# The second shifted copy of VectorE's key tiles made in place by an accumulating DMA, in a two-branch attention kernel with a planned order

## The chip, the cores and the metric

The kernel runs on one core of one Trainium2 chip. The metric is the device time of one execution in microseconds, as the median of several runs. The core has five engines that work side by side, each on its own in-order queue: TensorE (PE; PEld is its weight load), VectorE (DVE), ScalarE (ACT), GpSimd (POOL) and SyncE (SP, which here only issues DMAs).

## The reference

One input `x` of 2048 tokens by 512 goes through two attention branches, and a gate mixes the results. Branch A is linear attention; branch B is softmax attention, without a mask, with 32 heads of 16 columns:

```python
g = _sigmoid((x * gate_w).sum(-1, keepdims=True))
# A: phi(q), phi(k) = softmax(+-(q W)), softmax(+-(k W)); o = phi(q) (phi(k)^T v) / (phi(q) sum phi(k))
# B:
scores = jnp.einsum("bhqd,bhkd->bhqk", q, k) * (Dh ** -0.5)
p = _softmax(scores, axis=-1)
o = jnp.einsum("bhqk,bhkd->bhqd", p, v)
...
return g * a + (1 - g) * b
```

In branch B, 32 heads times 2048 x 2048 exponentials, 134 million, have to be taken. That is the bulk of the work.

## The kernel before

**Sets and key tiles.** Branch B is cut into 32 sets (`N_SETS`): four blocks of 512 queries, times four groups of eight heads, times two. A set holds four heads and 512 queries, and walks over 16 key tiles of 128 keys. For one key tile TensorE computes the scores of four heads into PSUM banks (L1231, `qk`), an engine turns them into exponentials in SBUF, and TensorE multiplies these by the values into the set's accumulator `psO` (L1282, `pv`), four matmuls for one round.

**Two engines take exponentials.** ScalarE does it with its exponential function, two instructions of 128 x 1024 a key tile, into an `E` tile (L1246, `exp`). VectorE has none. It takes a scaled score plus a bias as a 16-bit integer, so that the integer's bits, read as bf16, are roughly the exponential (L1251, `expd`, four instructions of 128 x 512 a key tile, into a `T` tile of 128 x 2048). To smooth the error of that, the kernel adds two shifted copies of the same integers: `T` plus 43 and `T` plus 85 (`SHIFT`), in two `TS` tiles, each multiplied by values that carry a weight of their own (`vS`). So a key tile of VectorE needs three rounds at L1282 (`T`, and twice `TS`), where one of ScalarE needs one round (`E`).

**Who makes the copies.** The first copy (43) is always VectorE's, one instruction of 128 x 2048 (L1263, `sh`). The second (85) is VectorE's or GpSimd's (L1266, `shp`): the planner picks one.

**The planner.** The order of all work on all engines is laid down when the program is built, by a scheduler in the file (`_Sched`). It gives each operation a duration (`occ`) and a latency, and places operations one after the other on the engine where they can start first. Whether a key tile goes to ScalarE or VectorE is open for the tiles in `DSET` (3, 5, 7, 9, 11, 13 in each set) and is decided as the plan grows. VectorE's tiles are offered in the order of `DSET`. `STYLES` is a table of random seeds, one for each 3 us of the plan, that vary the weights of these choices. The finished order is fixed; at run time an engine waits on semaphores wherever an instruction needs another engine's result, and everything queued behind it on that engine waits with it.

**The port rule in the planner.** VectorE's copies (kind `sh`) and GpSimd's operations are not allowed to overlap: each `sh` is planned after GpSimd's last operation, and each GpSimd operation waits for VectorE's last `sh` (`port`, and `o.deps.append(self.sh[-1])`).

**Buffers.** `T` tiles come from a ring of three, `TS` tiles from a ring of four. Of the eight PSUM banks one is `psO`; seven hold scores (`psR`): ScalarE takes them in pairs, VectorE one at a time. The same seven also serve the projections and branch A.

**Other work around it.** GpSimd also runs parts of branch A (L1080 to L1090), and weights the values for `vS` (L958). SP issues the transposing DMAs: at the end of a set `psO` is copied to `OT` by VectorE (L866), transposed by DMA to `OTT` (L1194), and normalised by VectorE (`rB` at L1172, `ob` at L1174).

Of the kernel before, what the change touches and what calls it, by code (L numbers as in the profile page):

```python
# [6 lines left out]
BF16 = mybir.dt.bfloat16  # L7
F32 = mybir.dt.float32
I16 = mybir.dt.int16
I32 = mybir.dt.int32  # L10
ACTF = mybir.ActivationFunctionType
ALU = mybir.AluOpType
# [12 lines left out]

VW = 18
NBANK = 7
DSET = (3, 5, 7, 9, 11, 13)
SHIFT = (0, 43, 85)
WB16 = (1.0, 0.79296875, 0.6328125)  # L30
ACC = 128.0 / math.log(2.0) * SCALE
# [13 lines left out]
NE_, NPH = 12, 6  # L45
WINDOW = 3.0
STYLES = (
# [14 lines left out]
LEAD = {"act": 1.1, "dve": 1.0}  # L62
NE = "dve"
PORT, LONG, NEAR, HOLD = 0.05, 0.8, 0.6, 3.0
SWITCH = 0.11
GAP, NEARBY = 0.02, 0.05
Q32, PSH, SHP = 1, 2, 1.88
PVS = 4.0
CONT = 3.0
PIECE = 4  # L70
DSTEP, DLAG = 3.6, 3.0
ND = lambda s: 6
HAM, CELLS = 3.413, 0.46
TOL0, TOL1, TOL2, TOL3 = 0.05, 0.1, 0.08, 0.1

# [33 lines left out]
class _Sched:  # L109
# [89 lines left out]
    def _earliest(self, o, at):  # L199
        if o.half is not None and self.last_mode == "row":  # L200
            at = max(max(self.rows[i] for i in o.half), self.last_start + GAP)
        if o.kind == "sh":
            at = max(at, self.port["pool"])
        elif o.eng == "pool" and self.sh:
            at = max(at, self.port["dve"], o.est)
            if o.occ > LONG and at > self.port["dve"] + NEAR:
                at = max(at, o.est + HOLD)
        return self._place(o, at)[0]
# [97 lines left out]
    def advance(self, until):  # L306
        ready, free, pend, order = self.ready, self.free, self.pend, self.order
        while self.left:
# [34 lines left out]
            if o.eng == "pe":  # L343
                sw = SWITCH if self.last_mode is not None and o.mode != self.last_mode else 0.0
                occ += sw
                self.last_mode = o.mode
                self.last_start = w + sw
                self.rows = [w + occ if o.half is None or i in o.half else max(x, self.last_start + GAP) for i, x in enumerate(self.rows)]
            elif o.eng == "pool":
                if self.sh and self.sh[-1] not in o.deps and self.sh[-1].end > w - 20.0:  # L350
                    o.deps.append(self.sh[-1])
                self.port["pool"] = w + occ + PORT
            elif o.kind == "sh":
                self.sh.append(o)
                self.port["dve"] = w + occ + PORT
# [160 lines left out]
def _general(fast):  # L516
# [8 lines left out]
        return _Slots(r.aps)  # L525

    xT, Wp, W_Av, WAT, kz, kvs = ns.xT, ns.Wp, ns.W_Av, ns.WAT, ns.kz, ns.kvs
    T = [x.bitcast(BF16) for x in ns.T_r.aps + ns.TS_r.aps]
    M_r = _Slots([ns.banks[:, i, :] for i in (4, 5, 6)])
    S_r = _Slots([ns.banks[:, 0:4, :]])  # L530
    st_r, ss_r = _Slots([x[:, 0, :] for x in ns.ss_r.aps]), _Slots([x[:, 1, :] for x in ns.ss_r.aps])
# [182 lines left out]
def _build(ctx, nc, A_x, A_wqkv, A_w_phi, A_wo, B_wqkv, B_wo, gate_w, out):  # L714
    cnt = [0]

    def sb(shape, dt=BF16, name="sb"):
        cnt[0] += 1
        return ctx.enter_context(nc.sbuf_tensor(f"{name}_{cnt[0]}", shape, dt))

    def ring(n, shape, dt=BF16, name="r"):
        return _Slots([sb(shape, dt, name)[:] for _ in range(n)])
# [26 lines left out]
    ct = sb([128, 112], F32, name="ct")  # L749
    flag = sb([128, 1], I32, name="flag")  # L750
    shc = sb([128, 2], I32, name="shc")

    qst_r = ring(2, [128, NQ], name="qst")
    qz_r = ring(2, [128, 4, NQ], name="qz")
    E_r = ring(NE_, [128, 1024], name="E")
    T_r = ring(3, [128, 2048], I16, name="T")
    TS_r = ring(4, [128, 2048], I16, name="TS")
    phk_r = ring(NPH, [128, 1024], name="phk")
    vA_r = ring(4, [128, 8, 66], name="vA")
    oAT_r = ring(2, [128, KT, NQ], name="oAT")  # L760
# [78 lines left out]
    z4 = pool(-99.3, 0.2, lambda e: e.tensor_tensor(ta, ta, tb, ALU.mult), [z3])  # L839
    op_qm = pool(-99.2, 0.2, lambda e: e.tensor_tensor(qmask[:], ta[:, 0:4], ta[:, 4:8], ALU.add), [z4])  # L840
    op_shc = [pool(-99.04, 0.1, lambda e, m=m: e.memset(shc[:, m:m + 1], SHIFT[m + 1] * 65537)) for m in range(2)]
    op_zeros = pool(-99.03, 0.1, lambda e: e.memset(zeros[:], 0.0))
    op_ones = pool(-99.05, 0.3, lambda e: e.memset(ones[:], 1.0))
    op_qz0 = [pool(-60, 1.8, lambda e: e.memset(qz_r.aps[1 - q_t[0, 0].idx], 0.0))]
# [358 lines left out]
    for s in range(N_SETS):  # L1203
# [12 lines left out]
        for eng, frac, kt in todo:  # L1216
            alt = (((s, kt), eng),) if kt in dset else ()
            pr = st_(s + frac)
            T, T1, T2 = (_Tile(T_r), _Tile(TS_r), _Tile(TS_r)) if eng == "dve" else (None, None, None)
            exps, es = [], []  # L1220
            for cc in range(2):
                rs = [_Tile(B_r), _Tile(B_r)]
# [32 lines left out]
            if eng == "act":  # L1255
                rounds = [(exps, lambda cc, es=es: es[cc].ap, lambda hd, kt=kt: vB[:, kt, hd, :], [], es)]
            else:
                di = DSET.index(kt)
                sh = []
                for m, X in ((1, T1), (2, T2)):  # L1260
                    two = m >= PSH
                    a2 = lambda eng: alt + ((("sh", s, kt, m), eng),) if two else alt
                    sh.append([add("dve", pr + 1.0 + 0.3 * m, 0.6, lambda e, T=T, X=X, m=m: e.tensor_single_scalar(  # L1263
                        X.ap, T.ap, SHIFT[m], ALU.add), deps=exps, tiles=[T, X], name="sh", kind="sh", alt=a2("dve"))])
                    if two:
                        sh[-1].append(pool(pr + 1.0 + 0.3 * m, SHP, lambda e, T=T, X=X, m=m: e.tensor_tensor(  # L1266
                            X.ap.bitcast(I32), T.ap.bitcast(I32), shc[:, m - 1:m].to_broadcast([128, 1024]), ALU.add),
                            exps + op_shc, "shp", [T, X], a2("pool")))
                s1, s2 = sh
                rounds = [(exps, lambda cc, T=T: T.ap[:, 1024 * cc:1024 * (cc + 1)].bitcast(BF16), lambda hd, kt=kt: vB[:, kt, hd, :], [], [T]),  # L1270
                          (s1, lambda cc, T=T1: T.ap[:, 1024 * cc:1024 * (cc + 1)].bitcast(BF16),
                           lambda hd, di=di: vS[:, 0, di, hd, :], [op_vS[g, kt // 4, 0]], [T1]),
                          (s2, lambda cc, T=T2: T.ap[:, 1024 * cc:1024 * (cc + 1)].bitcast(BF16),
                           lambda hd, di=di: vS[:, 1, di, hd, :], [op_vS[g, kt // 4, 1]], [T2])]
            for ri, (dps, rhs, lhs, more, holds) in enumerate(rounds):
                def pv(e, rhs=rhs, lhs=lhs, g=g, par=par, O=O, s=s, key=(kt, ri)):
                    ins = None
                    for cc in range(2):
                        for h in range(2):
                            col = 2 * h + cc  # L1280
                            hd = 8 * g + 4 * h + 2 * cc + par
                            ins = e.matmul(O.ap[32 * col:32 * col + VW, :], lhsT=lhs(hd), rhs=rhs(cc)[:, 512 * h:512 * (h + 1)],  # L1282
                                           start=(first_pv[s] == key), stop=(last_pv[s] == key), tile_position=(0, 32 * col),
                                           skip_group_check=True)
                    return ins
                o = add("pe", pr + 2.5 - 40.0 * (s == N_SETS - 1), 0.22, pv, deps=list(dps) + [ev_v[g, kt // 4], op_psO] + more, tiles=holds + [O], mode="col",
                        name=f"pv{s}.{kt}.{ri}", kind="pv", alt=alt)
                o.run = (s, (kt, ri))
                set_O[s] = O
                pvs.append(o)  # L1290
# [170 lines left out]
```

## Time and profile before

| | |
|---|---|
| Median of 3 runs | 707.38 us (706.78 to 709.51) |
| Profiled execution, first to last instruction | 707.6 us |
| ACT busy | 679.7 us (96%) |
| DVE busy | 667.4 us (94%) |
| PE busy | 657.1 us (93%) |
| POOL busy | 429.3 us (61%) |
| Granted TensorE clock, mean | 0.990 |

The profiler gives no time for the profiled execution other than its span, 707.6 us. It is 0.2 us above the median of the runs, so nothing has to be added to the span to compare it with them. Busy time counts the time in which an engine has an instruction in hand; instructions that follow each other without a gap overlap a little, so a group's busy time is less than its count times the mean duration. For sums, the busy time divided by the count is used.

### The profile page before, as it was taken

The page shows a single profiled execution, that of the slowest core. Times are in us where ns is not written, and L with a number is a line of the kernel's source. Part 1 is how long each engine was busy: PE and PEld are TensorE (multiplying, and loading weights), DVE is VectorE, ACT ScalarE, POOL GpSimd, SP SyncE. Part 2 cuts the span into 40 slices and gives each one's busy share as a digit, 9 for nine tenths or more (in the row PEclk, how much of TensorE's full clock was granted, in tenths as well). Part 3 has the DMA queues.
Part 4 walks back from the last instruction along what each step waited for, and adds up shares of the span by engine and source line. Part 5 has one row for each costly group of instructions (what it writes and reads, how often), then busy time and mean ns, then how long its engine had stood idle before and what let it go on. Part 6 is the DMA issues. An engine that isn't in the chain of part 4 may idle for free.

```text
span 707.6 us, 16129 instructions
## 1 busy us (share of the span) xinstructions
PE 657.1 (93%) x6632; PEld 208.6 (29%) x6632; DVE 667.4 (94%) x1191; ACT 679.7 (96%) x769; POOL 429.3 (61%) x364
## 2 busy tenths in 40 slices
PE   8999999999999999989999999999999999988895
PEld 3333343332322222222222322222222222222222
DVE  5998899999999999999999999999999999999995
ACT  6999799999999999999999999999999999999994
POOL 5468666655756656656667766666666755566541
PEclk9999899999999999999999999999999999999998
DMA  6501000011000000102111121112212111220001
GB/s 145 154 16 10 13 12 16 17 59 25 10 16 16 9 17 8 24 8 36 34 31 38 46 54 28 40 40 45 38 31 47 42 32 35 38 45 9 16 9 34
DMA packets 72192, 23.80 MB, mean 34 GB/s; under 512 B 64048, under 2 KB 72112, under 8 KB 72112
## 3 DMA queue, kind: packets, MB, share of 16 engines
q1 hardware_dynamic: 70896, 21.93, 14.7%
q8 instruction: 53, 0.87, 0.6%
q10 hardware_dynamic: 1216, 0.79, 0.4%
q14 instruction: 27, 0.22, 0.1%
HBM read 4.21 MB, written 2.10 MB: 9 GB/s over the span
## 4 chain that ended last, share of the span: by engine, by line
ACT 77%; PE 15%; DVE 5%; DMA 1%; issue 0%
ACT E L1246 73%; PE psR L1231 5%; PE psO L1282 4%; PE psR L883 3%; DVE T L1251 3%; ACT phk L1074 2%; ACT WAT L1074 2%; PE psR L1326 1%; PE psR L945 1%; DMA OTT<-OT 1%; DVE TS L1263 1%; PE psR L897 1%; PE psR L1023 0%; DVE vB L950 0%; PE psR L1006 0%
## 5 line engine op out<-in xcount | busy, mean ns | idle before, releaser
L1246 ACT ACTIVATE E<-psR 128x1024 bf16<-128x1024 f32 x692 | 649.1, 1118 | 12.0 <-PE psR L1231 10.9
L1251 DVE TENSOR_SCALAR T<-psR 128x512 int16<-128x512 f32 x664 | 424.1, 678 | 19.9 <-PE psR L1231 16.5
L1231 PE MATMUL psR<-qz,kT 32*128 32x512 bf16 (+1 forms) x2048 | 294.0, 386 | 39.9 <-ACT E L1246 27.9
L1266 POOL TENSOR_TENSOR TS<-T,shc 128x1024 int32<-128x1024 int32 x127 | 240.4, 1893 | 94.9 <-DVE TS L1263 78.1
L1231 PEld LDWEIGHTS psR<-qz,kT 32*128 32x128 bf16 (+1 forms) x2048 | 77.6, 91 | 292.3 <-ACT E L1246 212.7
L1263 DVE TENSOR_SCALAR TS<-T 128x2048 int16<-128x2048 int16 x205 | 137.0, 683 | 0.4
L1282 PE MATMUL psO<-E,vB 128*18 128x512 bf16 x1384 | 126.1, 385 | 0.1
L1282 PE MATMUL psO<-TS,vS 128*18 128x512 bf16 x1328 | 122.1, 384 | 0.0
L1282 PE MATMUL psO<-T,vB 128*18 128x512 bf16 x664 | 65.6, 386 | 0.0
L1090 POOL TENSOR_TENSOR phk<-phk,ss 128x1024 bf16<-128x1024 bf16 x16 | 30.9, 1929 | 31.9 <-DVE TS L1263 31.9
L1085 POOL TENSOR_TENSOR tr<-WAT 128x256 f32<-128x256 f32 x32 | 23.3, 729 | 37.8 <-DVE TS L1263 37.8
L1090 POOL TENSOR_TENSOR WAT<-WAT,ss 128x1024 bf16<-128x1024 bf16 x16 | 30.9, 1929 | 25.2 <-DVE TS L1263 25.2
L1282 PEld LDWEIGHTS psO<-TS,vS 128*18 128x18 bf16 x1328 | 29.9, 88 | 54.8 <-issue 38.2
L1282 PEld LDWEIGHTS psO<-E,vB 128*18 128x18 bf16 x1384 | 31.6, 88 | 44.4 <-issue 31.0
L883 PE MATMUL psR<-xT,WB 128*128 128x512 bf16 x128 | 33.2, 383 | 0.4 <-ACT WAT L1074 0.3
L883 PE MATMUL psR<-Wp,xT 128*128 128x512 bf16 x128 | 33.2, 382 | 0.0
L1080 POOL TENSOR_TENSOR WAT<-WAT 128x512 f32<-128x512 bf16 x16 | 18.5, 1155 | 21.2 <-DVE TS L1263 16.3
L1282 PEld LDWEIGHTS psO<-T,vB 128*18 128x18 bf16 x664 | 16.2, 88 | 20.9 <-issue 17.0
L866 DVE CAST OT<-psO 128x512 bf16<-128x512 f32 x31 | 21.1, 682 | 0.1
L958 POOL TENSOR_SCALAR vS<-vB 128x144 bf16<-128x144 bf16 (+1 forms) x32 | 11.9, 373 | 14.4 <-DVE TS L1263 12.2
L1080 POOL TENSOR_TENSOR WAT<-phk 128x512 f32<-128x512 bf16 x16 | 18.5, 1156 | 2.9 <-DVE TS L1263 2.3
L1086 POOL TENSOR_TENSOR tr<-tr 128x128 f32<-128x128 f32 x32 | 12.8, 400 | 11.0 <-DVE TS L1263 9.4
(114 smaller groups left out, 412.2 us busy)
## 6 DMA issues: line engine op xcount, KB each, us to landing
qz<-qst SPq DMA_DIRECT2D x120, 16.0 KB, 1.8
out_dram<-WAv SPq DMA_DIRECT2D x12, 128.0 KB, 1.7
WB<-in_B_wqkv_dram SPq DMA_DIRECT2D x3, 384.0 KB, 5.3
T<-in_A_x_dram SPq DMA_DIRECT2D x2, 256.0 KB, 4.4
T<-in_A_x_dram ACTq DMA_DIRECT2D x2, 256.0 KB, 4.7
WAv<-in_A_wqkv_dram SPq DMA_DIRECT2D x1, 512.0 KB, 6.6
WB<-in_A_wo_dram SPq DMA_DIRECT2D x1, 512.0 KB, 3.4
WB<-in_B_wo_dram SPq DMA_DIRECT2D x1, 512.0 KB, 3.6
```

Of the source, the lines that this page charges most:

```text
L866: return add("dve", prio, 0.6, lambda e: e.tensor_copy(dst(), src()), deps=deps, tiles=tiles, name=name)
L883: calls = [lambda e, t=t: e.matmul(tile.ap[:, off:off + 512], lhsT=lhs(t), rhs=rhs(t), start=(t == 0), stop=(t == KT - 1)) for t in range(KT)]
L1074: ex = [add("act", prio, 0.48, lambda e, s=s: e.activation(ev()[:, :, 16 * s:16 * s + 16], P(), ACTF.Exp, scale=1.0 - 2.0 * s), deps=[f] + ...
L1080: p1 = pool(prio + 2, 1.23, lambda e: e.tensor_tensor(v8(), eg()[:, :, 0:8], eg()[:, :, 8:16], ALU.add), ex + use_wat, tiles=[ee, tr], nam ...
L1085: p2 = pool(prio + 2, 0.92, lambda e: e.tensor_tensor(u4(), v8()[:, :, 0:4], v8()[:, :, 4:8], ALU.add), [p1], tiles=[tr, tr2])
L1090: return pool(prio + 6, 1.95, lambda e: e.tensor_tensor(eg(), eg(), ss.ap[:, 1, :].unsqueeze(2).to_broadcast([128, 64, DH]), ALU.mult), [o ...
L1231: ins = e.matmul(rs[h].ap, lhsT=kT[a:a + n, g, 128 * kt:128 * (kt + 1)], rhs=qt.ap[a:a + n, c, :], start=True, stop=True, tile_position=(a ...
L1246: exps.append(add("act", pr + 0.5 * cc, 0.905, lambda e, rs=rs, E=E: e.activation(E.ap.rearrange("p (a n) -> p a n", n=512), pair(rs), ACT ...
L1251: exps.append(add("dve", pr + 0.5 * cc + 0.01 * h, 0.6, lambda e, rs=rs, T=T, cc=cc, h=h: e.tensor_scalar(T.ap[:, 1024 * cc + 512 * h:1024 ...
L1263: sh.append([add("dve", pr + 1.0 + 0.3 * m, 0.6, lambda e, T=T, X=X, m=m: e.tensor_single_scalar(X.ap, T.ap, SHIFT[m], ALU.add), deps=exps ...
L1266: sh[-1].append(pool(pr + 1.0 + 0.3 * m, SHP, lambda e, T=T, X=X, m=m: e.tensor_tensor(X.ap.bitcast(I32), T.ap.bitcast(I32), shc[:, m - 1: ...
L1282: ins = e.matmul(O.ap[32 * col:32 * col + VW, :], lhsT=lhs(hd), rhs=rhs(cc)[:, 512 * h:512 * (h + 1)], start=(first_pv[s] == key), stop=(l ...
```

## The change

- `DSET` has seven key tiles a set (1, 3, 5, 7, 9, 11, 13) instead of six, so `vS` holds seven weighted value tiles.
- For key tiles 1, 3, 5 and 7 (`BYDMA`), the second shifted copy is no longer an instruction. Once the first round has read `T`, and once the first copy has been made from it, GpSimd issues a DMA that adds a constant row of 85s, held in DRAM, to `T` in place. The third round then reads `T`. The tile needs two buffers instead of three.
- For those tiles the first copy may be VectorE's or GpSimd's. For 9, 11 and 13 it stays as it was: the first is VectorE's, the second either's.
- `T` and `TS` become one ring of seven.
- The DMA's issue counts 1.1 us of GpSimd (`SDO`) and 5.0 us of latency (`SDL`) in the planner, and is left out of the port rule (`o.dma is None`).
- `STYLES` is a new table, of 233 entries; before it had 232.

```diff
-DSET = (3, 5, 7, 9, 11, 13)
+DSET = (1, 3, 5, 7, 9, 11, 13)
...
-Q32, PSH, SHP = 1, 2, 1.88
+Q32, PSH, SHP = 1, 1, 1.88
+SDO, SDL = 1.1, 5.0
+BYDMA = (1, 3, 5, 7)
...
-ND = lambda s: 6
+ND = lambda s: 7
...
-        elif o.eng == "pool" and self.sh:
+        elif o.eng == "pool" and o.dma is None and self.sh:
...
-            elif o.eng == "pool":
+            elif o.eng == "pool" and o.dma is None:
...
+    step = sb([128, 16], I16, name="step")
+    step_d = nc.dram_tensor("shift_row", [128, 16], I16, kind="Internal").ap()
...
-    T_r = ring(3, [128, 2048], I16, name="T")
-    TS_r = ring(4, [128, 2048], I16, name="TS")
+    T_r = ring(7, [128, 2048], I16, name="T")
...
+    op_st = pool(-99.035, 0.1, lambda e: e.memset(step[:], SHIFT[2]))
+    op_std = dma("sp", -90.0, 3.0, step_d, step[:], deps=[op_st], name="step")
...
+                add_dma = kt in BYDMA
+                both = 1 if add_dma else 2
+                s1, s2 = [], []
+                for m, X, got in ((1, T1, s1), (2, T2, s2))[:both]:
+                    a2 = lambda eng: alt + ((("sh", s, kt, m), eng),) if m == both else alt
+                    got.append(add("dve", pr + 1.0 + 0.3 * m, 0.6, lambda e, T=T, X=X, m=m: e.tensor_single_scalar(
                         X.ap, T.ap, SHIFT[m], ALU.add), deps=exps, tiles=[T, X], name="sh", kind="sh", alt=a2("dve")))
+                    if m == both:
+                        got.append(pool(pr + 1.0 + 0.3 * m, SHP, lambda e, T=T, X=X, m=m: e.tensor_tensor(
                             X.ap.bitcast(I32), T.ap.bitcast(I32), shc[:, m - 1:m].to_broadcast([128, 1024]), ALU.add),
                             exps + op_shc, "shp", [T, X], a2("pool")))
+                if add_dma:
+                    T2 = T
...
+                if ri == 2 and add_dma:
+                    dps = [add("pool", pr + 1.6, SDO, lambda e, T=T: e.dma_start(T.ap, step_d.rearrange("p n -> (p n)").unsqueeze(0).to_broadcast([128, 2048]), accum_op=ALU.add), deps=[pv0, op_std] + s1,
+                               tiles=[T], name="shd", dma=SDL, lane=lambda T=T, key=(s, kt): (("shd", T.idx), key), alt=alt)]
                 o = add("pe", pr + 2.5 - 40.0 * (s == N_SETS - 1), 0.22, pv, deps=list(dps) + [ev_v[g, kt // 4], op_psO] + more, tiles=holds + [O], mode="col",
                         name=f"pv{s}.{kt}.{ri}", kind="pv", alt=alt)
+                if ri == 0:
+                    pv0 = o
```

More of the change, by code (lines that the diff above doesn't have):

```diff
@@ L527, in _general @@
     xT, Wp, W_Av, WAT, kz, kvs = ns.xT, ns.Wp, ns.W_Av, ns.WAT, ns.kz, ns.kvs
-    T = [x.bitcast(BF16) for x in ns.T_r.aps + ns.TS_r.aps]
+    T = [x.bitcast(BF16) for x in ns.T_r.aps]
     M_r = _Slots([ns.banks[:, i, :] for i in (4, 5, 6)])
@@ L1218, in _build @@
             pr = st_(s + frac)
-            T, T1, T2 = (_Tile(T_r), _Tile(TS_r), _Tile(TS_r)) if eng == "dve" else (None, None, None)
+            T, T1, T2 = (_Tile(T_r), _Tile(T_r), _Tile(T_r)) if eng == "dve" else (None, None, None)
             exps, es = [], []
@@ L1258, in _build @@
                 di = DSET.index(kt)
[L1259 to L1266, printed above, removed]
+                add_dma = kt in BYDMA
[4 more added lines that the diff above has]
+                    got.append(add("dve", pr + 1.0 + 0.3 * m, 0.6, lambda e, T=T, X=X, m=m: e.tensor_single_scalar(
+                        X.ap, T.ap, SHIFT[m], ALU.add), deps=exps, tiles=[T, X], name="sh", kind="sh", alt=a2("dve")))
+                    if m == both:
+                        got.append(pool(pr + 1.0 + 0.3 * m, SHP, lambda e, T=T, X=X, m=m: e.tensor_tensor(
                             X.ap.bitcast(I32), T.ap.bitcast(I32), shc[:, m - 1:m].to_broadcast([128, 1024]), ALU.add),
                             exps + op_shc, "shp", [T, X], a2("pool")))
-                s1, s2 = sh
+                if add_dma:
+                    T2 = T
                 rounds = [(exps, lambda cc, T=T: T.ap[:, 1024 * cc:1024 * (cc + 1)].bitcast(BF16), lambda hd, kt=kt: vB[:, kt, hd, :], [], [T]),
@@ L1274, in _build @@
                            lambda hd, di=di: vS[:, 1, di, hd, :], [op_vS[g, kt // 4, 1]], [T2])]
+            o = None
             for ri, (dps, rhs, lhs, more, holds) in enumerate(rounds):
```

27 rows, old and new, of the table STYLES are left out of this document.

## The prediction

> **What bounds the kernel now.** I read the page's busy times first, then the busy times by stretch, the groups, the waits, and the DMA issues.
>
> ```profile
> span 707.6 us, 16129 instructions
> PE 657.1 (93%) x6632; PEld 208.6 (29%) x6632; DVE 667.4 (94%) x1191; ACT 679.7 (96%) x769; POOL 429.3 (61%) x364
> ACT 77%; PE 15%; DVE 5%; DMA 1%; issue 0%
> ```
>
> Three engines are within 3% of each other, and the chain that ended last lies on ACT for 77% of the span. An average hides the stages, so here are the same busy times in three stretches (columns: length, PE, PEld, DVE, ACT, POOL, granted clock, DMA share, GB/s). The first row is a short stretch that I use further down.
>
> ```profile
> core 0: us, PE busy (x) PEld busy (x) DVE busy (x) ACT busy (x) POOL busy (x), PEclk, DMA share, GB/s
> 153.80:157.30 3.50, 3.50 (x46) 1.62 (x48) 3.31 (x7) 3.24 (x4) 1.53 (x3) 1.00 0.50 152
> ...
> 0.00:150.00 150.00, 143.47 (x1471) 56.47 (x1471) 134.56 (x239) 135.64 (x151) 94.02 (x103) 0.98 0.20 45
> 150.00:650.00 500.00, 466.13 (x4700) 138.18 (x4699) 485.38 (x870) 496.37 (x567) 312.94 (x251) 1.00 0.15 32
> 650.00:707.00 57.00, 47.52 (x472) 13.91 (x464) 47.46 (x84) 47.67 (x54) 22.32 (x12) 0.97 0.07 18
> ```
>
> From 150 to 650 us ACT is busy 496.4 of 500 us, and DVE 485.4. There, time falls only if exponentials leave ACT, and DVE has no room to take them unless something leaves DVE. In the first 150 us PE is the fullest, 143.5 against 135.6 for ACT. There, moving key tiles to DVE, which need more rounds of PE, gains nothing.
>
> ```profile
> L1246 ACT ACTIVATE E<-psR 128x1024 bf16<-128x1024 f32 x692 | 649.1, 1118 | 12.0 <-PE psR L1231 10.9
> L1251 DVE TENSOR_SCALAR T<-psR 128x512 int16<-128x512 f32 x664 | 424.1, 678 | 19.9 <-PE psR L1231 16.5
> ...
> L1266 POOL TENSOR_TENSOR TS<-T,shc 128x1024 int32<-128x1024 int32 x127 | 240.4, 1893 | 94.9 <-DVE TS L1263 78.1
> ...
> L1263 DVE TENSOR_SCALAR TS<-T 128x2048 int16<-128x2048 int16 x205 | 137.0, 683 | 0.4
> L1282 PE MATMUL psO<-E,vB 128*18 128x512 bf16 x1384 | 126.1, 385 | 0.1
> ```
>
> ACT's 692 instructions are 346 key tiles at 2 x 649.1/692 = 1.876 us. DVE's 664 are 166 tiles, 5.2 of the six offered in each of 32 sets, at 4 x 424.1/664 = 2.555 us. The 332 copies are split 205 on DVE, at 137.0/205 = 0.668 us, and 127 on GpSimd, at 1.893 us. A round of four matmuls at L1282 costs 4 x 126.1/1384 = 0.364 us of PE.
>
> **What the change takes off DVE.** VectorE's tiles are offered in the order of `DSET`, and the first four of the seven are now the DMA's. A set took 5.2 tiles, so I count all four in every set: 128 DMAs. With N tiles on DVE, and P copies on GpSimd, DVE keeps (N - 128) first copies of tiles 9 to 13 and N - P of the copies that either may make: S = 2N - 128 - P. How large P stays is decided by GpSimd's queue.
>
> ```profile
> POOL TS L1266 <- DVE TS L1263: 78.1, 53, 5.3
> ...
> POOL phk L1018 <- DVE TS L1263: 8.7, 4, 2.7
> ```
>
> These are the first and the last of nine rows of GpSimd's waits on DVE's copies; together they hold 236 of the 278 us that GpSimd is idle (707.6 - 429.3). They come from the port rule, which the next fence shows at work: DVE's copy ends at 303.51, and GpSimd's, which had been waiting 1.17 us, starts.
>
> ```profile
> 302.83 0.68 DVE L1263 TENSOR_SCALAR TS<-T 128x2048 int16<-128x2048 int16 x1
> ...
> 303.60 1.89 POOL L1266 TENSOR_TENSOR TS<-T,shc 128x1024 int32<-128x1024 int32 x1 [1.17 <-DVE TS L1263]
> ```
>
> GpSimd issues no DMA before, so the issue's price has to be bounded, by a load that SP issues (ns, min/median/max, and its start):
>
> ```profile
> L795 SPq DMA_DIRECT2D WB<-in_A_wo_dram x1: 391/391/391, 153.8 to 153.8; - x1
> ```
>
> SP's issue takes 0.39 us, and GpSimd's own pass over such a tile takes 1.89. I take the planner's 1.1, which lies between: 128 x 1.1 = 141 us, with 50 and 242 as ends. GpSimd's other work is 429.3 - 240.4 = 188.9 us, and the seventh weighted value tile adds about 2. If all idle time stays, 707.6 - 188.9 - 141 - 278.3 = 99 us are left, which hold 52 copies; if the waits shrink as DVE's copies do, all 127 fit. I take P = 90. With x tiles moved from ACT, S = 2(166 + x) - 128 - 90 = 114 + 2x. DVE's time is then 667.4 - 0.668(91 - 2x) + 2.555x = 606.6 + 3.891x, and ACT's 679.7 - 1.876x. They meet at x = 12.7, at 655.9 us: 23.8 us less. With P = 52 the same sum gives 15.5 us less, with P = 127 it gives 31.8. It counts only from 150 to 650 us, 71% of the span: **-17 us**, ends -11 and -23.
>
> PE gets two rounds more for each moved tile: 13 x 2 x 0.364 = 9 us. Its 50 idle us hide them, most of which lie after 150 us. The memset of the constant row, its store by SP at the start and the one-tile-longer `vS` cost nothing on the path: they stand before the first `T` tile needs them. The ring: before, a tile used three of seven buffers; now `T` is held through the DMA, but needs only one beside it. I count it at nothing; if it binds, DVE's next exponential waits, and the gain goes (a rival below).
>
> **What it adds to the path.** PE's queue is in order. The third round of a DMA tile now waits for a landing, and the scores for ACT and DVE are queued behind it. How much lateness can PE hide?
>
> ```profile
> PEld psR L1231 <- ACT E L1246: 212.7, 492, 0.9
> ...
> PEld psO L1282 <- DVE TS L1263: 4.6, 19, 0.5
> ...
> PEld psO L1282 <- POOL TS L1266: 3.0, 11, 0.4
> ```
>
> PE reaches the next scores 212.7/492 = 0.43 us ahead of the bank that ACT frees. So about 0.4 us of lateness is free, and the rest lands on ACT, which is never idle in this stretch. Now only 30 of 332 rounds on `TS` find their copy late, by 0.25 us. That works because the engines repeat themselves: the copies' durations (ns, min/median/max) hardly vary, while transfers do.
>
> ```profile
> L1263 DVE TENSOR_SCALAR TS<-T x205: 622/682/807, 16.6 to 695.0; 128x2048 int16<-128x2048 int16 x103
> L1266 POOL TENSOR_TENSOR TS<-T,shc x127: 1887/1892/1899, 13.4 to 692.5; 128x1024 int32<-128x1024 int32 x127
> ```
> ```profile
> WAv<-in_A_wqkv_dram SPq DMA_DIRECT2D x1, 512.0 KB, 6.6
> WB<-in_A_wo_dram SPq DMA_DIRECT2D x1, 512.0 KB, 3.4
> WB<-in_B_wo_dram SPq DMA_DIRECT2D x1, 512.0 KB, 3.6
> ```
>
> One accumulating DMA writes 128 x 2048 x 2 bytes, 512 KB, the size of these three loads. They landed 3.4, 3.6 and, among other loads, 6.6 us after issue. The first of them is the stretch from 153.8 in the table above: a DMA share of 0.50 for 3.5 us, so one such copy holds the 16 engines for 1.75 us. An accumulation has to read its destination as well. Counted as a second pass, that gives 3.4 + 1.75 = 5.2 us at best and 6.6 + 1.75 = 8.4 when others are under way. The plan allows 1.1 + 5.0 = 6.1. So landings lie between 0.9 us early and 2.3 late. I take a quarter of them late by 1 us, since quiet times are the rule (DMA share 0.15): 128 x 0.25 x (1.0 - 0.4) = **+19 us**; the ends are 0 and 128 x 1.9 = 243.
>
> The transfers also get in the way of others. 128 x 1.75 to 3.5 us is 224 to 448 us, a DMA share of 0.32 to 0.63 on top of 0.15. The set's last step rests on a transposing DMA:
>
> ```profile
>   DMA OTT<-OT: 1.0, 2
> ...
> DMA to landing us min/median/max: 2.3/2.3/4.2
> ```
>
> DVE waited for it twice in 31 sets, and its landing is nearly always 2.3 us. If half of the 31 meet an accumulation, and are held for half of 1.75 us, DVE stands 14 us; I let a third of it through to the end: **+5 us**, ends 0 and 14.
>
> GpSimd's queue gets waits as well: an issue waits for the first round of its tile and for the first copy, and the copies and branch A's steps stand behind it. In the plan that is in order, and a delay of GpSimd alone is seen by PE only through the copies (the 11 late rounds above); I count it at nothing, ends 0 and 10.
>
> One thing is left out of the port rule: an issue may now fall on a copy of DVE. With S = 139 copies of 0.68 us in 700, an issue of 1.1 us meets one with a chance of 139 x 1.78/700 = 0.35, 45 times in all. Nothing before shows such a meeting; it costs from nothing to 0.68 us, and I count it at nothing, ends 0 and 30. The Trainium skill, "SBUF — State Buffer", section "Who interferes with whom", says that a VectorE instruction in a two-port mode and GpSimd shut each other out for the whole instruction, and that descriptor writing for GpSimd's DMAs is stopped by it; by that rule the 45 meetings would cost about 45 x 0.34 = 15 us, partly on the path, and the sum would be some 722. No trace so far shows it.
>
> The sum, against the span of 707.6: -17 + 19 + 5 = +7, so 714.6; the median of the runs is 0.2 below the span: **714 us**.
>
> **Rivals.**
>
> *The DMA keeps to the plan (faster).* If the landings stay at 5.2 us, nothing is late, and the saving on DVE shows: 707 - 17 = 690, ends 684 and 696. For it: the two quiet loads of 3.4 and 3.6. Against it: the 6.6, and that the accumulations themselves raise the DMA share to about 0.5 to 0.8. The point from which it decides: fewer than one landing in five over 0.4 us late. By the Trainium skill, "DMA: Bandwidth & Descriptors", section "Anatomy of one DMA — SWDGE (gpsimd) path", a DMA takes some 2.0 us plus its bytes at 436 GB/s; as an estimate with two reads that is 4.4 us, inside the plan, and the time would be that of this rival. The loads of 3.4 and 3.6 stand near that page's 3.2 for one read. Chance 0.33.
>
> *The plan does not get shorter.* If the ring of seven, or PE in its fullest stretches, stops DVE from taking more tiles, the copies leave DVE and it idles; or fewer than 128 tiles go by DMA. Small loss and small gain cancel: 707, 704 to 711. For it: PE at 143.5 of 150 us early on. Against it: PE's 34 idle us of the 500 later. Chance 0.13.
>
> *Every landing is late.* If reading one row 128 times over, or adding, is slow, a landing comes at 7.5 us, 1.4 late each time. 1.0 us of that is beyond the cover; if half the rounds have been planned later than they must, 64 us follow: 707 - 17 + 64 = 754, and more for slower landings. For it: no row shows an accumulation. Against it: the 5.2 of the nearest rows. Chance 0.13.
>
> **How the numbers follow.** My forecast, 714, has 0.41; its own range is 705 to 730, where 13% to 45% of the landings are late by that 1 us. A measurement of this kernel can tell about 0.5% from no change, 3.5 us. Below 704: the first rival, 0.33. Between 704 and 711: the second rival, 0.13. Above 711: the forecast and the last rival, 0.54. The range takes in most of the first rival, and ends short of the last: 686 to 745.
>
> **What would show it.** Right: 128 DMA issues on GpSimd's queue; DVE's copies down from 205 to about 140, and tiles on DVE up from 166 to about 179; ACT's share below 96%; new waits of PE at L1282 on a DMA into `T` of some tens of us; ACT waiting for scores more than 10.9 us. Wrong: no such waits of PE (the first rival), waits of over 60 us or landings over 7 us (the last), or tiles on DVE still near 166 (the second).

## The result, and the profile after

| | before | after |
|---|---|---|
| Median of 4 runs (lowest to highest) | 707.94 us (706.78 to 709.51) | 810.65 us (809.06 to 812.89) |
| Span of the profiled execution | 707.6 us | 811.0 us |
| Granted TensorE clock, mean | 0.990 | 0.918 |

The changed kernel is slower: the ratio of the times is 1.1443, 95% interval 1.1404 to 1.1482, or 103 us. The forecast was 714, its range ended at 745. Where the runs of one kernel lay more than 1.5% apart (the plain copy in experiment 2 and the first kernel of experiment 4), its time and ratio leave out the runs that were over 1.5% above its fastest.

The page's first part, and the chain that ended last (by engine, then by line):

```profile
span 811.0 us, 16329 instructions
...
PE 676.1 (83%) x6652; PEld 210.1 (26%) x6724; DVE 657.1 (81%) x1164; ACT 665.9 (82%) x743; POOL 508.2 (63%) x470
...
PE 33%; ACT 24%; DMA 22%; DVE 9%; issue 6%; POOL 4%; SPq 1%; POOLq 0%
ACT E L1250 22%; DMA T<-shift_row 15%; PE psR L1235 12%; PE psO L1289 10%; DVE T L1255 6%; PE psR L887 4%; DMA Wp<-WAT 4%; PE psR L1338 2%; PE psR L949 2%; DMA OTT<-OT 1%; POOL T L1294 1%; ACT phk L1078 1%; DVE T L1268 1%; SPq L935 1%; DMA oBT<-ob 1%
```

No engine is full any more. ACT's share of the chain fell from 77% to 24%, and DMA's rose from 1% to 22%. The work was split between the engines about as planned, as the groups show (line numbers moved up by four to seven):

```profile
L1250 ACT ACTIVATE E<-psR 128x1024 bf16<-128x1024 f32 x666 | 631.6, 1058 | 124.5 <-PE psR L1235 116.3
L1255 DVE TENSOR_SCALAR T<-psR 128x512 int16<-128x512 f32 x716 | 456.3, 681 | 60.1 <-PE psR L1235 54.0
...
L1271 POOL TENSOR_TENSOR T<-T,shc 128x1024 int32<-128x1024 int32 x105 | 199.4, 1908 | 103.2 <-PE psO L1289 79.5
...
L1294 POOL DMA_DIRECT2D T<-shift_row x127 | 121.5, 974 | 65.8 <-PE psO L1289 49.7
...
L1268 DVE TENSOR_SCALAR T<-T 128x2048 int16<-128x2048 int16 x126 | 86.1, 691 | 9.4 <-PE psO L1289 9.2
```

716/4 = 179 key tiles are VectorE's, 13 more than before, and its copies fell from 205 to 126. But ACT, which had waited 10.9 us for scores, now waits 116.3. Who holds PE up is in the waits (total us, times, longest):

```profile
DVE rA L1158 <- PE psR L1154: 42.4, 8, 13.4
PEld psO L1289 <- DMA T<-shift_row: 41.9, 35, 3.5
PE psO L1289 <- DMA T<-shift_row: 30.2, 25, 3.2
...
PE psR L1154 <- issue: 24.9, 3, 12.7
...
PE psR L1154 <- DMA Wp<-WAT: 14.7, 3, 6.1
...
DVE rB L1176 <- DMA OTT<-OT: 6.3, 3, 5.2
```

Two kinds of wait are new. PE waits for the accumulating DMA into `T` (PEld and PE wait together, so the two rows are not to be added), and at L1154 for branch A's transposing DMA into `Wp`. The 24.9 us put down to "issue" are of that second kind in their longest case too, as the timeline around it shows, with the busy times of that stretch (PE, PEld, DVE, ACT, POOL, granted clock, DMA share, GB/s):

```profile
353.43 1.23 POOL L1294 DMA_DIRECT2D T<-shift_row  x1
353.50 4.58 SPq L1148 DMA_TRANSPOSE Wp<-WAT  x1
...
371.99 0.61 PE L1154 MATMUL psR<-kz,Wp 128*128 128x68 bf16 x8 [12.72 <-issue]
```
```profile
362.00:371.00 9.00, 0.00 (x0) 0.00 (x0) 0.00 (x0) 0.00 (x0) 0.51 (x2) 0.58 0.86 60
```
```profile
issues: line engine op xcount, KB each, median us to landing
T<-shift_row POOLq DMA_DIRECT2D x1, 512.0 KB, 18.3
qz<-qst SPq DMA_DIRECT2D x4, 16.0 KB, 11.5
Wp<-WAT SPq DMA_TRANSPOSE x1, 18.4
```

The last fence is the DMA view of the window from 353 to 372 us, where "us to landing" is the median. An accumulation and a transposing DMA were issued 0.07 us apart. Both landed only 18.3 and 18.4 us later, just before PE moved again at 371.99; SP's issue took 4.58 us instead of 1.23. For 9 us PE, DVE and ACT did nothing, while the DMA engines were recorded as 86% busy and moved 60 GB/s.

It is not the only such meeting. Here is another, again put down to "issue":

```profile
440.83 0.98 POOL L1294 DMA_DIRECT2D T<-shift_row  x1
441.01 1.25 SPq L1148 DMA_TRANSPOSE Wp<-WAT  x1
...
452.94 0.27 PE L1154 MATMUL psR<-kz,Wp 128*128 128x68 bf16 x2 [6.18 <-issue]
```

By the trace's landing times, all six of PE's waits in the two rows at L1154 (24.9 and 14.7, together 39.6 us) end within 0.14 us of a landing in `Wp`. Of the 16 transposes into `Wp`, six were issued within 0.2 us of an accumulation. They landed after 5.4 to 18.4 us. Nine of the other ten landed after 3.0 to 4.4. So `Wp` is late mainly where the plan issues its transpose together with an accumulation.

The accumulation's own row, then the landings of branch A's transposes into `Wp` (L1148) and `oAT` (L1167), in three answers of the view by line:

```profile
L1294 POOL DMA_DIRECT2D T<-shift_row x127: 831/877/1645, 24.2 to 792.5; - x127
...
DMA to landing us min/median/max: 4.9/6.5/18.3
```
```profile
L1148 SPq DMA_TRANSPOSE Wp<-WAT x16: 1232/1284/4577, 337.8 to 716.3; - x16
...
DMA to landing us min/median/max: 3.0/4.4/18.4
```
```profile
L1167 SPq DMA_TRANSPOSE oAT<-WAv x16: 1190/1202/2149, 347.0 to 726.3; - x16
...
DMA to landing us min/median/max: 2.4/5.3/10.5
```

Before, these two landed in 3.0/3.1/4.9 and 2.4/2.7/3.7 us. The page's DMA queue row says that the accumulations took 47.1% of the 16 engines' span: 0.471 x 811/127 = 3.0 us of all of them for each.

### The profile page after: what moved, and what is told of

Its sections match the earlier page's. It is cut to its first block, busy times and chain, and to the rows that moved or that the text cites. A ratio compares the mean times of both kernels' runs of the same rounds, so it can differ in the third digit from the quotient of the medians.

```text
span 811.0 us, 16329 instructions
## 1 busy us (share of the span) xinstructions
PE 676.1 (83%) x6652; PEld 210.1 (26%) x6724; DVE 657.1 (81%) x1164; ACT 665.9 (82%) x743; POOL 508.2 (63%) x470
## 3 DMA queue, kind: packets, MB, share of 16 engines
q0 software_dynamic: 18288, 66.59, 47.1%
## 4 chain that ended last, share of the span: by engine, by line
PE 33%; ACT 24%; DMA 22%; DVE 9%; issue 6%; POOL 4%; SPq 1%; POOLq 0%
ACT E L1250 22%; DMA T<-shift_row 15%; PE psR L1235 12%; PE psO L1289 10%; DVE T L1255 6%; PE psR L887 4%; DMA Wp<-WAT 4%; PE psR L1338 2%; PE psR L949 2%; DMA OTT<-OT 1%; POOL T L1294 1%; ACT phk L1078 1%; DVE T L1268 1%; SPq L935 1%; DMA oBT<-ob 1%
## 5 line engine op out<-in xcount | busy, mean ns | idle before, releaser
L1250 ACT ACTIVATE E<-psR 128x1024 bf16<-128x1024 f32 x666 | 631.6, 1058 | 124.5 <-PE psR L1235 116.3
L1255 DVE TENSOR_SCALAR T<-psR 128x512 int16<-128x512 f32 x716 | 456.3, 681 | 60.1 <-PE psR L1235 54.0
L1271 POOL TENSOR_TENSOR T<-T,shc 128x1024 int32<-128x1024 int32 x105 | 199.4, 1908 | 103.2 <-PE psO L1289 79.5
L1289 PE MATMUL psO<-T,vS 128*18 128x512 bf16 x1432 | 140.3, 408 | 31.1 <-DMA T<-shift_row 30.2
L1294 POOL DMA_DIRECT2D T<-shift_row x127 | 121.5, 974 | 65.8 <-PE psO L1289 49.7
L1268 DVE TENSOR_SCALAR T<-T 128x2048 int16<-128x2048 int16 x126 | 86.1, 691 | 9.4 <-PE psO L1289 9.2
L1289 PE MATMUL psO<-T,vB 128*18 128x512 bf16 x716 | 72.7, 396 | 0.2 <-DVE T L1255 0.2
L1289 PEld LDWEIGHTS psO<-T,vS 128*18 128x18 bf16 x1432 | 31.8, 89 | 102.1 <-issue 50.4
L1154 PE MATMUL psR<-kz,Wp 128*128 128x68 bf16 x128 | 7.7, 210 | 40.8 <-issue 24.9
L1084 POOL TENSOR_TENSOR WAT<-phk 128x512 f32<-128x512 bf16 x16 | 18.8, 1176 | 13.8 <-DVE ob L1178 8.3
L1338 PE MATMUL psR<-WB,oAT 128*128 128x512 bf16 x51 | 16.8, 439 | 10.9 <-issue 6.4
```

Of the source, the lines that this page charges most:

```text
L1084: p1 = pool(prio + 2, 1.23, lambda e: e.tensor_tensor(v8(), eg()[:, :, 0:8], eg()[:, :, 8:16], ALU.add), ex + use_wat, tiles=[ee, tr], nam ...
L1250: exps.append(add("act", pr + 0.5 * cc, 0.905, lambda e, rs=rs, E=E: e.activation(E.ap.rearrange("p (a n) -> p a n", n=512), pair(rs), ACT ...
L1255: exps.append(add("dve", pr + 0.5 * cc + 0.01 * h, 0.6, lambda e, rs=rs, T=T, cc=cc, h=h: e.tensor_scalar(T.ap[:, 1024 * cc + 512 * h:1024 ...
L1268: got.append(add("dve", pr + 1.0 + 0.3 * m, 0.6, lambda e, T=T, X=X, m=m: e.tensor_single_scalar(X.ap, T.ap, SHIFT[m], ALU.add), deps=exps ...
L1271: got.append(pool(pr + 1.0 + 0.3 * m, SHP, lambda e, T=T, X=X, m=m: e.tensor_tensor(X.ap.bitcast(I32), T.ap.bitcast(I32), shc[:, m - 1:m]. ...
L1294: dps = [add("pool", pr + 1.6, SDO, lambda e, T=T: e.dma_start(T.ap, step_d.rearrange("p n -> (p n)").unsqueeze(0).to_broadcast([128, 2048 ...
```

## The experiments

Two theories at the start. *Late landing*: the third rounds wait for their own DMA, and everything queued behind them on PE too. *Contention*: the accumulations hold the DMA engines, and transfers that others wait for land late. A third, that the new plan itself is worse, is tested first.

**1. The plan without the DMA.** Each accumulation becomes a memset of 128 x 1; order, buffers and waits stay. The second shift is left out.

```diff
     sch.run()
+    scr = sb([128, 8], I32, name="scr")
+    for i, o in enumerate(o for o in sch.ops if o.name == "shd"):
+        o.dma, o.lane, o.fn = None, None, lambda e, i=i: e.memset(scr[:, i % 8:i % 8 + 1], 0)
```

> The changed kernel with its plan kept; each accumulating DMA is a 0.1 us memset of GpSimd on a scratch word, with the same waits before it, so the third round of those tiles reads T without the second shift. Theory 1 (transfers: the accumulating DMAs and the transposing DMAs hold each other up, and TensorE stands behind both): 700 to 708 us, TensorE's waits at L1154 and on T from DMA gone. Rival (the new plan itself is worse: ring of seven, three rounds on more tiles): 740 us or more, with the waits of GpSimd on TensorE still there.

702.62 us, ratio 0.9915 (0.9889 to 0.9941).

```profile
PE 641.0 (92%) x6652; PEld 207.4 (30%) x6724; DVE 651.9 (93%) x1164; ACT 659.1 (94%) x743; POOL 400.8 (57%) x470
```

The plan is sound, but it gains 6 us at the most, with a DMA that costs nothing. The 108 us between this run and the changed kernel are the DMA's doing: its issue, its own landing, and what it does to other transfers. All losses below are counted from 702.6.

**2. Smaller transfers, and plain ones.** One kernel accumulates 512 of the 2048 columns only (the rest of the second shift is left out); another overwrites `T` with the row instead of adding (`<row>` stands for the constant row).

```diff
-e.dma_start(T.ap, <row>.to_broadcast([128, 2048]), accum_op=ALU.add)
+e.dma_start(T.ap[:, 0:512], <row>[0:512].to_broadcast([128, 512]), accum_op=ALU.add)   # quarter
+e.dma_start(T.ap, <row>.to_broadcast([128, 2048]))                                     # copy
```

> The changed kernel; the accumulating DMA covers only 512 of T's 2048 columns (128 KB instead of 512), the rest of the second copy is left unshifted. If the time that the accumulations hold the DMA engines counts: landing about 3.5 us, time 705 to 715, near the run without DMA. If the number of DMAs and their issue count: 770 or more.

709.4 us, ratio 1.0016 (0.9994 to 1.0038).

> The changed kernel; GpSimd's DMA writes the constant row over T instead of adding it, so that T's third round reads constants. Same bytes written, no read of the destination. If the second pass over the destination is what makes the transfers long: DMA share of that queue down from 47% to about 28%, landing 4.5 us at the median, time 715 to 740. If a software-queue DMA of 512 KB beside transposes is enough in itself: 780 or more.

736.7 us, ratio 1.0364 (1.032 to 1.0408). The queue rows, the quarter's first (packets, MB, share of 16 engines), and each kernel's row of the accumulation or copy:

```profile
q0 software_dynamic: 18288, 16.65, 18.8%
...
T<-shift_row POOLq DMA_DIRECT2D x127, 128.0 KB, 4.0
```
```profile
q0 software_dynamic: 18288, 66.59, 29.4%
...
T<-shift_row POOLq DMA_DIRECT2D x127, 512.0 KB, 4.8
```

The quarter has the same 127 issues on GpSimd, in the same places, and its landing shows in no wait of PE on `T`; it loses 7 us. So the issues and the added dependencies are cheap, and the size of the transfer is not. The plain copy holds the engines for 0.294 x 741.3/127 = 1.7 us, so reading one row of DRAM over and over is not slow; adding makes it 3.0. The copy lands in time, at 4.8 us, with direct waits of 7.7 us of PEld, and still loses 34 us. Late landing cannot be the whole.

**3. Every second accumulation.** As in 1, for every second one in GpSimd's order.

> The changed kernel; every second accumulating DMA is a 0.1 us memset on a scratch word, its tile's third round reads T unshifted. If the loss grows with the number of DMAs alone: half of 108 us, 755. If it comes from DMAs that queue behind one another and behind transposes (share of the engines 47% now, 24% then): much less than half, 705 to 725, the landing near its least value of 4.7 us.

741.94 us, ratio 1.0471 (1.0433 to 1.051): with a share of 25.9% of the engines a loss of 39 us, beside 34 at 29.4% (copy) and 7 at 18.8% (quarter). The time lies between the two that were expected. PEld's direct waits on `T` are down to 3.9 us. Branch A's remain: PE waits 9.2 and 4.2 us at L1154.

**4. The accumulations elsewhere.** They write two spare tiles (2000 columns) that nobody reads; the third rounds read `T` without waiting for a DMA, so the second shift is left out. `vS` has one set instead of two, to make room.

```diff
+    for i, o in enumerate(shds):
+        o.fn = lambda e, i=i: e.dma_start(spare[i % 2], <row>, accum_op=ALU.add)
+        o.deps = o.deps + ([shds[i - 2]] if i >= 2 else op_spare)   # and taken out of all other deps
```

> The changed kernel with its plan kept; the same accumulating DMAs at the same places of GpSimd's queue, 2000 of 2048 columns, but into two spare tiles, and no round of TensorE waits for them (an issue waits for the landing of the one before the last). The third round reads T unshifted, and second and third round share one set of weighted values. It leaves what the transfers do to others, without what TensorE waits for their own landing. The run with no DMA was 702.6, with a plain copy of the same size 740, the change 811. If the direct waits carry most of the loss: 715 to 740. If the transfers' harm to others carries it: 770 or more.

778.1 us, ratio 1.099 (1.0888 to 1.1092), from runs of 772.61 and 783.58. With nobody waiting for the accumulations, 75 of the 108 us stay; by the interval it is 69 to 83. Some of that is the edit's own: here GpSimd waits 22.5 us for a spare tile, which it doesn't in the changed kernel, and PE then 7.4 us for GpSimd's copies (both from the profile of a run of 785.76 us). The same with a plain copy:

> As the run that sends the DMAs elsewhere, with transposes kept, but the DMAs are plain copies instead of accumulations: 1.7 us of the 16 engines each instead of 3.0. If the loss is set by how long each DMA holds the engines: 735 us or below, as with the plain copy over T (740), and transposes land nearer to 3 us. If it is the number of DMAs or their issue: near 785.

733.53 us, ratio 1.035 (1.0296 to 1.0404): 31 of the copy's 34 us stay. What the transfers do to others is the larger part in both.

**5. Plain copies in place of the transposing DMAs.** Four transfers (into `Wp`, `oAT`, `OTT`, `oBT`) move the same bytes without transposing, so their elements arrive in another order; `psO` starts at 1 instead of 0.

```diff
-e.dma_start_transpose(ptt.ap, ph.ap)
+e.dma_start(ptt.ap.rearrange("p g q -> p (g q)"), ph.ap)     # and the other three likewise
```

> The changed kernel, accumulating DMAs kept; the four kinds of transposing DMA on SP (branch A's phT and oAT, branch B's otT and oBT) are plain copies of the same bytes, so nothing is transposed; the accumulator's idle rows start at 1 instead of 0. Theory 1a (what is slow is a transposing and an accumulating DMA in flight together): 720 to 740 us, landing of T under 6 us at the median and its longest under 10, TensorE's idle time at L1154 under 5 us. Theory 1b (any transfer beside the accumulations is late, and the accumulations alone miss their plan): 780 us or more, little changed. Rival (new plan): 780 or more.

786.53 us, ratio 1.1057 (1.0978 to 1.1136). PE's long wait at L1154 is gone, the direct waits on `T` are not:

```profile
PEld psO L1289 <- DMA T<-shift_row: 46.6, 47, 2.1
...
DVE rA L1158 <- PE psR L1154: 7.4, 5, 3.4
```

24 us come back, not the 70 to 90 that were expected if only a transposing and an accumulating DMA slowed each other. The longest landing of an accumulation falls from 18.3 to 10.2 us, the median does not fall (6.7, from 6.5). Of the four plain transfers into `Wp` that were issued within 0.2 us of an accumulation, three landed after 2.3 to 2.6 us. Both edits together (4 and 5):

> The two edits together: the accumulating DMAs go to two spare tiles with no round waiting for them, and the four kinds of transposing DMA are plain copies. Each edit alone gave 785 to 787 us, against 811 for the change and 703 with no DMA, so the two losses overlap. If the waits for T's landing and for the slowed transposes are all there is: 703 to 725 us. If the accumulations slow any transfer on SP's queue, plain copies and the q loads too, and TensorE waits for those: 750 us or more.

758.97 us, ratio 1.0744 (1.0717 to 1.0771). The two edits give 33 and 24 us alone and 52 together. Within the intervals (some 7 and 6 us for the first two) they add up, so these are in the main two separate losses. 56 us stay with neither. There the plain transfers still land late, at medians of 4.7 and 5.0 us where the fastest take 2.4 and 2.0:

```profile
oAT<-WAv SPq DMA_DIRECT2D x16, 128.0 KB, 4.7
...
oBT<-ob SPq DMA_DIRECT2D x15, 128.0 KB, 5.0
```

PE's waits there show who is held (L1340 is the output projection, which reads `oAT` and `oBT`):

```profile
PE psR L1340 <- issue: 14.4, 9, 5.0
...
PE psO L1291 <- POOL T L1273: 8.6, 8, 2.1
...
PE psR L1340 <- DMA oBT<-ob: 3.7, 1, 3.7
```

The four longest waits at L1340, 17.1 us, each end 0.5 us after a landing in `oAT` or `oBT`.

**6. The third round later.** If PE reaches these rounds too early, moving them back in its queue helps. Each was moved by up to 6 us, behind rounds that were planned after it.

```diff
+    for o in reversed(moved):          # pv operations that depend on an accumulation
+        ...
+            pe.insert(j, pe.pop(i))     # up to 6 us later in PE's order
```

> The changed kernel, nothing left out; in TensorE's queue each third round that waits for an accumulating DMA is moved behind rounds up to 6 us later, as far as no circle of waits arises (127 rounds, 240 us in all, 1.9 us each). If landings later than planned are what costs, and a landing at 6.5 us instead of 6.1 with a tail is covered by 1.9 us: 740 to 770 us, TensorE's waits on T from DMA under a third of the 72 us. If the harm to other transfers or the tail of the landings carries the loss: 790 or more.

876.88 us, ratio 1.2379 (1.2319 to 1.2439): slower still. The direct wait is nearly gone, and others have taken its place:

```profile
POOL T L1271 <- PE psO L1289: 110.2, 38, 9.2
...
DVE T L1268 <- PE psO L1289: 58.8, 25, 16.5
...
DVE T L1255 <- PE psO L1289: 39.1, 31, 4.1
...
PEld psO L1289 <- DMA T<-shift_row: 5.5, 6, 1.9
```

DVE's exponentials and copies now wait for PE to give `T` tiles back: the ring of seven binds. In the changed kernel the second and third of these rows are 9.2 and 3.5 us.

**7. One half of the time each.** As in 1, for the accumulations planned after 350 us, and for those before. In the changed kernel branch A's transposes run from 338 us on.

> The accumulations planned before 350 us stay (59 of 127), the later ones are replaced by a tiny memset (their second shift is left out). In the kernel after, ACT lost some 11 us of busy time against e1 in the first 350 us, where none of branch A's two kinds of transposing DMA is under way, and some 70 after it. Theory (the loss is made where accumulations and branch A's transposes share the DMA engines): 710 to 720 us. Rival (the loss follows the number of accumulations, wherever they are): 108 x 59/127 = 50 over e1's 702.6, some 753 us.

730.43 us, ratio 1.0329 (1.0303 to 1.0356).

> The other half: the 68 accumulations planned after 350 us stay, the earlier ones are replaced by a tiny memset (their second shift is left out). Theory (the loss is made where accumulations and branch A's transposes share the DMA engines): 785 to 800 us, nearly the whole loss with half the accumulations. Rival (the loss follows their number): 702.6 + 108 x 68/127 = some 760 us. If both halves come out far below these, the loss needs both, through the delay that the first half carries into the second.

792.83 us, ratio 1.1224 (1.1176 to 1.1271). Busy times by stretch (columns as in the stretches before; ACT's is the fourth), for experiment 1, for the early half, for the late half and for the changed kernel:

```profile
150.00:350.00 200.00, 185.31 (x1967) 58.83 (x1983) 194.10 (x343) 197.08 (x230) 125.12 (x151) 1.00 0.10 22
350.00:500.00 150.00, 137.04 (x1421) 42.26 (x1434) 142.36 (x256) 146.69 (x165) 90.33 (x97) 1.00 0.20 40
```
```profile
150.00:350.00 200.00, 181.81 (x1894) 57.67 (x1916) 187.97 (x327) 190.22 (x220) 151.72 (x148) 0.97 0.61 114
350.00:500.00 150.00, 131.65 (x1334) 40.77 (x1350) 133.29 (x242) 137.53 (x155) 85.36 (x90) 0.98 0.30 53
```
```profile
150.00:350.00 200.00, 185.34 (x1959) 58.81 (x1979) 194.33 (x343) 197.31 (x231) 124.98 (x152) 1.00 0.10 22
350.00:500.00 150.00, 113.05 (x1076) 33.27 (x1089) 108.49 (x193) 112.19 (x125) 86.87 (x71) 0.89 0.70 105
```
```profile
150.00:350.00 200.00, 181.35 (x1926) 58.24 (x1946) 190.18 (x331) 192.27 (x223) 152.40 (x152) 0.99 0.62 116
350.00:500.00 150.00, 113.38 (x1018) 32.11 (x1035) 102.90 (x185) 105.87 (x118) 82.49 (x69) 0.83 0.72 102
```

From 150 to 350 us the DMA engines are 61% busy with the early half, and ACT loses 7 us of 197 to it. From 350 to 500, with 70%, it loses 34.5 of 146.7. The 59 early accumulations cost 28 us, 0.47 each; the 68 late ones cost 90, 1.33 each. The late half came out inside the 785 to 800 us that were expected if the loss is made beside branch A's transfers. The early half met neither value: it costs more than the 10 or so us of ACT's time that I had read off, partly because its last accumulations and their delay reach into the next stretch (ACT loses 9 us there). But the loss does not follow the number. It is made mainly in the stage in which branch A's transfers run; the accumulations themselves land later there too (median 7.8 us in the late half, 5.9 in the early one). That is a place and not yet a cause. With plain transfers in place of the transposes (experiment 5) ACT is busy 122.2 us from 350 to 500, so it still loses 24.5 of 146.7, against 40.8 in the changed kernel. What else in this stage makes an accumulation dear was not separated. The two halves' losses add up to 118, near the 108 of the whole.

## Why the prediction was wrong

**The step that failed is the transfers that get in the way of others: +5 us, where some 75 stay when nobody waits for the accumulations (experiment 4).** The prediction worked out that the accumulations would hold the DMA engines for a third to two thirds of the time; 47.1% was measured. From that it then priced one transfer, `OTT` at the set's end, which it had seen DVE wait for. That one was nearly harmless: its median landing went from 2.3 to 2.4 us, and DVE waits 6.3 us for it. The transposes of branch A and of the output (`Wp`, `oAT`, `oBT`), and the loads into `qz`, showed next to no wait before (`Wp` cost PE 0.6 us), and so weren't priced. A transfer that nobody waits for at a DMA share of 0.15 isn't one that nobody waits for at 0.7; `Wp` was late above all where it was issued together with an accumulation. PE's queue is in order, so a late `Wp` stops scores and rounds for both exponential engines at once: PE's two rows at L1154 are 39.6 us. The 75 us left in experiment 4 (which hold some waiting of the edit's own) are the size of this step, the 24 of experiment 5 the part that goes with transposing.

**A term was missing: PE's own speed.** The spans of experiment 1 and of the changed kernel differ by 110.5 us. PE's busy time differs by 35.1 of these (641.0 and 676.1), for the same 6652 matmuls: one of the scores takes 406 ns in the mean instead of 386, and the mean granted clock is 0.918 instead of 0.988. The other 75 are PE standing still: 39.6 at L1154, 30.2 for the accumulations, some 10 at the output projection (L1338) and 4.7 for `qz`, less shorter waits for ACT. This divides PE's time; it doesn't say what the span would be without one of the parts.

**The landing, +19 us, was the right mechanism and somewhat small.** 6.5 us in the middle lies in the stated 5.2 to 8.4; the fastest, 4.9, lies below it, and the slowest, 18.3, far above. The weight loads of 35 of the 127 rounds wait for their accumulation, 28% where a quarter was taken, and by 1.2 us each (41.9/35) where 0.6 was counted. Taking the wait away gave back 33 us (experiment 4), and 28 on top of experiment 5. The engine time of one accumulation, 3.0 us, lies in the stated 1.75 to 3.5. By the Trainium skill, "DMA: Bandwidth & Descriptors", section "Anatomy of one DMA — SWDGE (gpsimd) path", the estimate with two reads was 4.4 us; the fastest landing, 4.9, stands near it. By it nothing would have been late, and the time that of the faster rival; the median of 6.5 shows how far landings beside other transfers lie above it.

**The saving, -17 us, was too large by 11.** VectorE's side came out as worked: 127 DMAs, 126 copies against the 139, 179 tiles as forecast. In experiment 1 DVE is busy 651.9 and ACT 659.1 us, against 655.9 for both. But the span fell by 7 only: of ACT's 20.6 us of saved work 13.5 came back as idle time (700.5 - 659.1 = 41.4, before 27.9). The rival "the plan does not get shorter" was nearer the truth in that step.

**Counted at nothing.** The ring: GpSimd's copies wait 79.5 us for PE to give `T` tiles back (35.4 in experiment 1, 6.5 before), but PE's weight loads wait only 2.4 us for these copies, and DVE's copies and exponentials 12.7 (9.2 and 3.5) for a tile. So the ring costs little in the kernel as it is, and experiment 6 shows that it binds as soon as tiles are held longer. The port: DVE's copy took 691 ns in the mean against 683, 126 x 0.008 = 1.0 us in all. But the issues suffer, as here:

```profile
181.82 1.36 POOL L1294 DMA_DIRECT2D T<-shift_row  x1
...
182.42 0.68 DVE L1268 TENSOR_SCALAR T<-T 128x2048 int16<-128x2048 int16 x1
```

The issue ends at 183.18, 0.08 us after DVE's copy, and takes 1.36 us where the median is 0.88. In 26 of the 127 issues a copy begins 0.15 to 0.63 us after the issue does, and 25 of these issues end 0.08 to 0.13 us after that copy. The mean of all is 0.974 us, so 127 x (0.974 - 0.877) = 12.3 us of GpSimd's time go into issues longer than the median. The Trainium skill's rule in "SBUF — State Buffer", section "Who interferes with whom", from which 15 us were worked out, is borne out in kind and nearly in size. It hardly reaches the time of the kernel: the quarter's issues are as long (969 ns in the mean), and it loses 7 us with all its issues and new waits. There were 65 meetings of an issue and a copy, more than the 45 worked out.

**The rivals.** Slower was the likelier side at 0.54, but the rival for much slower rested on landings at 7.5 us and gave 754. The median landing is 6.5. Its price came from the wrong place, and no rival had a transfer of another branch as its mechanism. The signs named for "right" all came true: 127 issues, 126 copies, 179 tiles, ACT's share at 82%, PE's waits on `T` of some tens of us, ACT waiting longer. They test the saving and the landing, and none of them tests the +5.

**Still open.** The 56 us that are left with both edits (4 and 5) can be read but weren't taken apart by a run. PE's busy time is 22.6 us above that of experiment 1 (663.6, at a granted clock of 0.954); the output projection waits 18.1 us for late transfers, and PE 8.6 for GpSimd's copies, some of it the edit's own. The granted clock was 0.58 in the stretch where PE stood still; whether such stops are what slows PE's matmuls afterwards wasn't tried. Why the two transfers issued at 353 us took 18 us, and why a transpose suffers from an accumulation issued with it, the trace doesn't say.

No run points to a version that beats the kernel before: even with a DMA that costs nothing, and with part of the work left out, this plan is only 0.85% faster.

## What to carry to other kernels

Before moving an engine's work to DMA, work out the DMA share that results, and then go through every transfer in the kernel that an in-order queue waits for, also those that show no wait today; their landing times were measured on quiet engines. Look too for transfers that the order issues at the same moment. Read the waits and the share by stage: the same accumulations cost 0.47 us each in one half and 1.33 in the other. And run the plan with the new operation emptied first: it gives the ceiling, here 6 us, which tells at once how little contention the change can afford.

## What was not expected of the hardware

An accumulating DMA of 512 KB held the 16 engines for 3.0 us where a plain copy of the same size and source held them 1.7, and its issue took 0.88 us of GpSimd in the median where that of the plain copy took 0.58. An accumulation and a transposing DMA issued 0.07 us apart landed after 18.3 and 18.4 us, beside medians of 6.5 and 4.4, while the engines were recorded as 86% busy at 60 GB/s. Six transposes into `Wp` issued within 0.2 us of an accumulation took 5.4 to 18.4 us. In the quarter kernel the six so placed took 4.3 to 5.1, and as plain transfers three of four took 2.3 to 2.6.
